# DeltaNet and a hard-swish MLP in one kernel: weight pieces loaded in one transfer or in several slabs

## The chip, the cores and the metric

The kernel runs on one core of a Trainium2 chip. A core has five engines, each with an instruction queue of its own: TensorE (PE, matrix products, with PEld for the loading of the stationary operand), VectorE (DVE), ScalarE (ACT), GpSimd (POOL) and SyncE (SP), which here does nothing but issue DMA transfers. The transfers run on 16 DMA engines. The time is that of the device in microseconds; the kernel before has a median of 661.7 us over three runs (661.16 to 663.97).

## The reference

Two parts in a row. The first is a delta-rule recurrence over 768 steps, for 4 batches of 8 heads of width 48; the second is an MLP over the 3072 tokens.

```python
for t in range(S):
    kt, vt, bt = (k_n[:, :, t], v[:, :, t], beta[:, :, t, None])
    y[:, :, t] = np.einsum('bhd,bhde->bhe', q[:, :, t], state)
    v_old = np.einsum('bhde,bhd->bhe', state, kt)
    state = state + bt[:, :, :, None] * np.einsum('bhd,bhe->bhde', kt, vt - v_old)
...
x = np.ascontiguousarray(attn_out.transpose(0, 2, 1, 3)).reshape(B * S, H * D)
h = x @ w_in                                   # (3072, 384) @ (384, 2048)
g = h * np.clip(h + 3.0, 0.0, 6.0) / 6.0
out = g @ w_out                                # (3072, 2048) @ (2048, 384)
```

`k_n` is k divided by its norm per token and head. q, k, v and beta are float32. The two weight matrices are float64 in memory, 8 bytes an element, and the kernel makes float32 of them itself.

## The kernel before

**The recurrence.** The 768 steps are cut into 24 chunks of 32 tokens. A tile has 128 rows: 32 tokens of each of the 4 batches. For each chunk k is normalised (`norms`: a square on ACT at L396, a sum on DVE at L402, and so on), k and q are transposed by PE (L513) and copied by ACT (L521, tile `KQ`), products of them become a triangular matrix (PE L536, DVE L547), which is inverted; for the first chunk `product` does that by matrix products (L585 and the lines around it), for groups of four chunks DVE does it column by column after a transposition (L458). Then the state is read, corrected and updated, and the output y of the chunk is turned into `xT`, the MLP's input.

**The MLP.** `up` multiplies two chunks (a block of 256 tokens) by w_in (L983), applies the activation, and `down` multiplies by w_out. Later blocks use variants with fewer products (L1055, L1215).

**The weights.** Both matrices are loaded in pieces, eight of w_in and eight of w_out, 768 KB of float64 each. Piece i of w_in is 256 columns of all 384 rows: 128 partitions, three row blocks (`s`), 256 columns. Piece i of w_out is two row blocks of 128 rows with all 384 columns. `load_w(i)` (L309) issues the transfer of piece i from SP at L320, into a home in `spare` or in a part of `w_out` that is not yet in use; pieces from 6 on reuse a home, and so wait until the piece that had it has been read. `scales` reads the raw halves of a piece on ACT in four operations (L345); `convert` reads them on DVE in three (L367, L372, L378) and writes float32. The first ACT operation and the first two DVE operations of a piece read the raw data; all of them take the whole piece at once. The MLP's first product (L983) needs the first pieces of w_in.

**The other loads.** For each chunk there are four transfers of 48 KB each for k (L168), q (L180) and v (L193), one for each batch, all issued from SP. The output is written from SP as well (L1140).

**What sets the order.** The first part of the program is emitted by the list `ORDER`, a hand-written sequence of words; each word takes one step of one generator: `w` issues the next weight piece, `k`, `q` and `v` one transfer of 48 KB, `a` one operation of `scales`, `c` one of `convert`, `n` of the norms, and so on. The order of the words is the order of each engine's queue. `W` is `w` with an added wait: `do` looks for the one instruction that the step emitted and has `behind_tensor` make it wait for the latest PE instruction before it. In the list, piece 12 alone is issued by `W`. After the list, a loop over the remaining chunks follows a plan of its own, with no weight loads in it.

The lines that the change touches are L320 to L322 in `load_w` and the few lines in `do` for the words K, Q, V and W.

Of the kernel before, what the change touches and what calls it, by code (L numbers as in the profile page):

```python
# [10 lines left out]
U32 = mybir.dt.uint32  # L11
# [33 lines left out]
def kernel(  # L45
# [21 lines left out]
    nc = tc.nc  # L67
# [27 lines left out]
    def rows(b):  # L95
        return slice(C * b, C * b + C)
# [4 lines left out]
    def group(t):  # L101
        return (0, t) if t < G0 else ((t - G0) // GS + 1, (t - G0) % GS)
# [34 lines left out]
    def needs(*what):  # L137
        assert past.issuperset(what), (what, set(what) - past)
# [70 lines left out]
    for j, value in enumerate((1.0, -1.0)):  # L209
        m = mask2[:, j, :]  # L210
        for b in range(B):
            nc.gpsimd.memset(mask2[rows(b), j, :], value)
            nc.gpsimd.affine_select(
                out=mask2[rows(b), j, :], in_=mask2[rows(b), j, :], pattern=[[1, C]],
# [88 lines left out]
    raws = []  # L303
    for i, n in enumerate((0, 1, 2, 3, 4, 5, 0, 1, 3, 4, 5, 0, 1, 5, 0, 1)):
        s, f = weights[i][0].shape[1:]
# [3 lines left out]
    def load_w(i):  # L309
        dst, src = weights[i]  # L310
        if src.dtype == FP32:
            if i >= NWI:
                needs(("w", NWI - 1))
            nc.sync.dma_start(out=dst, in_=src)
            past.add(("raw", i))
            return
        if i in frees:
            needs(("seen", frees[i], 0), ("seen", frees[i], 1))
        past.add(("raw", i))
        nc.sync.dma_start(  # L320
            out=raws[i].rearrange("p s f z -> p s (f z)"), in_=src.bitcast(U32)
        )  # L322

    es = [
        spare[:, 2, j : j + WP * NKT // 2].bitcast(U16).rearrange("p (s f) -> p s f", s=NKT)
# [1016 lines left out]
    def made(name, make, ok=True):  # L1342
        if name not in gens:
            gens[name] = make() if ok else iter(())
        return gens[name]

    def prep_of(t):
        return made(("p", t), lambda: prep(t), t < N)
# [7 lines left out]
    def inverse_of(g):  # L1356
        return made(
            ("i", g), lambda: halves_of(g) if g == 1 else inverse(g), g < NG
        )
# [6 lines left out]
    def pieces():  # L1366
        for i in range(NW):
            load_w(i)
            yield
# [37 lines left out]
    def behind_tensor(ins):  # L1407
        last = next(
            i for i in reversed(nc.cur_bb.bb.instructions) if i.engine == mybir.EngineType.PE
        )  # L1410
        tc.add_manual_dep(
            ins, last.name,
            mybir.DependencyInfo(mybir.DependencyClass.Sync, mybir.DependencyReason.DATA),
            reason="held back",
        )

    def do(word):
        if word in ("K", "Q", "V", "W"):
            n = len(nc.cur_bb.bb.instructions)
            next(gens[word.lower()])  # L1420
            (new,) = nc.cur_bb.bb.instructions[n:]
            behind_tensor(new)
        elif word in gens:
            next(gens[word])
        elif word[0] == "r":
            relus[word[1]].pop(0)()
        elif word[0] == "g":
            pending[word[1]].pop(0)()
        elif word == "e":
            evicts.pop(0)()  # L1430
        elif word[0] == "i":
            next(inverse_of(int(word[1:])), None)
        else:
            name, t = word[0], int(word[1:])
            if name == "p" and t >= LS + LE:
                next(prep_of(t), None)
            else:
                key = (name, t) if name in "hp" else ("early", name, t)
                next(made(key, lambda: makers[name](t)), None)

    with tc.manual_schedule():
        for word in ORDER.split():
            word, _, n = word.partition("*")
            for _ in range(int(n or 1)):
                do(word)
# [12 lines left out]
        for t in range(LS, N):  # L1458
            g, i = group(t)
# [94 lines left out]
```

## Time and profile before

| What | Value |
|---|---|
| median of three runs | 661.7 us (661.16, 661.7, 663.97) |
| the profiled execution | 662.71 us, of which its span 661.0 |
| PE busy | 632.6 us, 96% of the span |
| DVE, ACT, POOL busy | 499.5, 263.2, 226.6 us |
| transfers of weight pieces | 16 of 768 KB; median 4.9 to 7.0 us to landing, by group |
| transfers of k, q, v | 96 each, of 48 KB; median 3.0, 2.6, 2.5 us to landing |
| granted TensorE clock | mean 0.989; 0.50 in 32 to 40 us |

The span runs from the first to the last instruction. Times in the profile are in microseconds from its start. L12 is line 12 of the kernel. SPq is SP's queue, which is not counted as busy; for a transfer the profile gives the start and length of its issue, and for most the time from issue to landing. `spare<-in_moe_w_in_dram` is the transfer of a piece of w_in into the tile `spare`; the names kf, qb and vf are the tiles of k, q and v. In the slices, each digit is the busy share in tenths of one fortieth of the span.

### The profile page before, as it was taken

What the parts mean: (1) busy time and instruction counts of PE and PEld (TensorE: products, weight loads), DVE (VectorE), ACT (ScalarE), POOL (GpSimd) and SP (SyncE); (2) the same over time, 40 slices, a digit from 0 to 9 for tenths busy, and PEclk for the clock granted to TensorE, in tenths of its full rate; (3) what the DMA queues carried; (4) which work ended last, traced back from release to release, by engine and by line L of the source; (5) the groups of instructions that cost most, each with busy time, mean ns of one, the idle gap of its engine ahead of it and who ended that gap; (6) DMA issues with size and microseconds to landing.
All of it is one profiled execution on the core that took longest, in us unless ns stands there. A gap on an engine that the chain in (4) does not pass through costs nothing.

```text
span 661.0 us, 26631 instructions
## 1 busy us (share of the span) xinstructions
PE 632.6 (96%) x11640; PEld 568.8 (86%) x11640; DVE 499.5 (76%) x1164; ACT 263.2 (40%) x547; POOL 226.6 (34%) x352
## 2 busy tenths in 40 slices
PE   2768999999999999999999999999999999999997
PEld 2658987776689989999999999999999999999997
DVE  5899877798657988758988748979658998456354
ACT  4786578322232154154144244244244144153240
POOL 5531023003661354453254354164152241331330
PEclk9979999999999999999999999999999999999999
DMA  7888246212041030041030030030020020000101
GB/s 171 210 216 217 76 100 165 49 25 39 16 84 20 2 75 3 3 83 28 3 74 3 2 74 3 2 63 2 3 50 2 2 49 3 23 18 2 26 1 24
DMA packets 88692, 33.28 MB, mean 50 GB/s; under 512 B 80224, under 2 KB 83424, under 8 KB 88576
## 3 DMA queue, kind: packets, MB, share of 16 engines
q1 hardware_dynamic: 88224, 31.29, 21.5%
q8 instruction: 91, 1.49, 0.9%
q10 hardware_dynamic: 352, 0.30, 0.2%
q14 instruction: 25, 0.20, 0.1%
HBM read 26.84 MB, written 4.72 MB: 48 GB/s over the span
## 4 chain that ended last, share of the span: by engine, by line
PE 91%; DVE 3%; DMA 2%; ACT 2%; SPq 1%; issue 1%; ACTq 0%; DVEq 0%
PE po L1215 28%; PE ph L1055 27%; PE ph L983 9%; PE po L1151 6%; PE ks L795 4%; PE pz L816 3%; PE pt L513 3%; PE py L816 3%; PE su L927 3%; PE sc L536 3%; ACT spare L345 1%; PE yt L862 1%; DMA w_out<-in_moe_w_in_dram 1%; SPq L168 1%; PE pi L673 1%
## 5 line engine op out<-in xcount | busy, mean ns | idle before, releaser
L1055 PE MATMUL ph<-xT,w_in 128*128 128x128 f32 (+1 forms) x720 | 156.7, 321 | 0.2 <-issue 0.2
L1019 POOL TENSOR_TENSOR g<-g 128x256 f32<-128x256 f32 (+1 forms) x144 | 88.0, 612 | 105.5 <-ACT g L1069 99.9
L1055 PEld LDWEIGHTS ph<-xT,w_in 128*128 128x128 f32 x720 | 116.9, 191 | 6.7
L1215 PE MATMUL po<-w_out,g 128*128 128x192 f32 x640 | 110.6, 326 | 0.0
L1215 PEld LDWEIGHTS po<-w_out,g 128*128 128x128 f32 x640 | 104.6, 190 | 0.5
L1215 PE MATMUL po<-spare,g 128*128 128x192 f32 x480 | 86.7, 332 | 0.0
L1069 ACT ACTIVATE g<-ph 128x512 f32<-128x512 f32 x72 | 43.0, 597 | 107.5 <-PE ph L1055 107.5
L1215 PEld LDWEIGHTS po<-spare,g 128*128 128x128 f32 x480 | 77.2, 190 | 1.8
L983 PE MATMUL ph<-xT,w_in 128*128 128x128 f32 (+1 forms) x384 | 72.8, 339 | 1.5 <-ACT xT L866 0.6
L1225 POOL TENSOR_TENSOR o<-o,u 128x192 f32<-128x192 f32 x18 | 14.9, 828 | 163.5 <-ACT o L1222 76.1
L983 PEld LDWEIGHTS ph<-xT,w_in 128*128 128x128 f32 x384 | 60.2, 196 | 9.0 <-DVE g L993 0.9
L1082 DVE TENSOR_TENSOR g<-ph,g 128x256 f32<-128x256 f32 x72 | 30.2, 419 | 47.3 <-PE ph L1055 44.8
L748 DVE TENSOR_TENSOR pr<-A 128x30 f32<-128x30 f32 (+9 forms) x150 | 57.6, 384 | 3.3
L1201 DVE TENSOR_TENSOR g<-g 128x512 f32<-128x512 f32 x80 | 55.3, 712 | 3.6 <-PE po L1215 3.6
L1102 DVE SCALAR_TENSOR_TENSOR g<-o,g 128x512 f32<-128x512 f32 x72 | 52.5, 729 | 7.2 <-ACT o L1099 7.2
L753 DVE TENSOR_TENSOR A<-A,pr 128x30 f32<-128x30 f32 (+9 forms) x150 | 55.1, 367 | 3.3
L1055 PE MATMUL ph<-beta_tok,sums_in 128*128 128x128 f32 x288 | 55.9, 275 | 0.1
L1099 ACT ACTIVATE o<-g 128x512 f32<-128x512 f32 x72 | 45.4, 631 | 12.0 <-DVE g L1102 8.5
L345 ACT ACTIVATE spare<-spare 128x768 uint16<-128x768 uint16 (+1 forms) x56 | 47.3, 850 | 3.2 <-DMA kf<-in_k_dram 1.7
L499 POOL TENSOR_TENSOR kb<-kf,inv 128x384 f32<-128x384 f32 x24 | 21.7, 906 | 75.5 <-issue 42.6
L1222 ACT ACTIVATE o<-po 128x192 f32<-128x192 f32 x40 | 13.2, 330 | 83.2 <-PE po L1215 83.2
L1151 PE MATMUL po<-w_out,g 128*128 128x384 f32 x128 | 45.4, 490 | 0.0
(137 smaller groups left out, 1010.2 us busy)
## 6 DMA issues: line engine op xcount, KB each, us to landing
kf<-in_k_dram SPq DMA_DIRECT2D x96, 48.0 KB, 3.0
qb<-in_q_dram SPq DMA_DIRECT2D x96, 48.0 KB, 2.6
vf<-in_v_dram SPq DMA_DIRECT2D x96, 48.0 KB, 2.5
out_dram<-o SPq DMA_DIRECT2D x90, 48.0 KB, 1.6
spare<-in_moe_w_in_dram SPq DMA_DIRECT2D x4, 768.0 KB, 5.3
w_out<-in_moe_w_in_dram SPq DMA_DIRECT2D x4, 768.0 KB, 5.6
w_out<-in_moe_w_out_dram SPq DMA_DIRECT2D x4, 768.0 KB, 7.0
spare<-in_moe_w_out_dram SPq DMA_DIRECT2D x4, 768.0 KB, 4.9
```

The source lines that it names most:

```text
L345: nc.scalar.activation(out=z, in_=z if n else d.bitcast(I16)[:, :, :, 3], func=func, bias=value, scale=scale,)
L748: nc.vector.tensor_tensor(out=pv, in0=A[:, j + 1 :, j].unsqueeze(2).to_broadcast([n, w, j]), in1=A[:, j, 0:j].unsqueeze(1).to_broadcast([n ...
L753: nc.vector.tensor_tensor(out=A[:, j + 1 :, 0:j], in0=A[:, j + 1 :, 0:j], in1=pv, op=ALU.subtract)
L983: nc.tensor.matmul(ph[:, cols], lhsT=w_in[:, s, f * 128 : (f + 1) * 128], rhs=xT[:, s, cols], start=(s == 0), stop=(s == NKT - 1),)
L1019: nc.gpsimd.tensor_tensor(out=out, in0=a, in1=b, op=op)
L1055: nc.tensor.matmul(ph[:, n], lhsT=w, rhs=x, start=start, stop=stop, skip_group_check=True)
L1069: nc.scalar.activation(out=gt, in_=ph[:], func=ACTF.Copy)
L1099: nc.scalar.activation(out=r, in_=g, func=ACTF.Relu, bias=0.5, scale=1.0 / 6.0)
L1102: nc.vector.scalar_tensor_tensor(out=g, in0=r, scalar=1.0, in1=g, op0=ALU.min, op1=ALU.mult)
L1151: nc.tensor.matmul(pos[c][:], lhsT=gs[blk, f // 2][:, f % 2, c * P : (c + 1) * P], rhs=w_out[:, f, :], start=(f == 0), stop=(f == NFC - 1),)
L1201: nc.vector.tensor_tensor(out=A(f, *out, 4), in0=A(f, *a, 4), in1=A(f, *b, 4), op=op)
L1215: nc.tensor.matmul(ps[n][:], lhsT=A(f - f % 2, *a)[:, f % 2], rhs=b[:, f], start=(f == 0), stop=(f == HF - 1),)
```

## The change

`load_w` takes the views of destination and source that it had and issues one transfer for each index of their second dimension: three for a piece of w_in (one for each block of 128 rows, 256 KB each) and two for a piece of w_out (384 KB each). All go to SP's queue one after the other, within one step of the generator. `do` for the words with an added wait now gives that wait to each instruction that the step emitted. What is read afterwards, and the list `ORDER`, stay as they are.

```diff
         if i in frees:
             needs(("seen", frees[i], 0), ("seen", frees[i], 1))
         past.add(("raw", i))
-        nc.sync.dma_start(
-            out=raws[i].rearrange("p s f z -> p s (f z)"), in_=src.bitcast(U32)
-        )
+        dst, src = raws[i].rearrange("p s f z -> p s (f z)"), src.bitcast(U32)
+        for j in range(dst.shape[1]):
+            nc.sync.dma_start(out=dst[:, j], in_=src[:, j])
...
         if word in ("K", "Q", "V", "W"):
             n = len(nc.cur_bb.bb.instructions)
             next(gens[word.lower()])
-            (new,) = nc.cur_bb.bb.instructions[n:]
-            behind_tensor(new)
+            for new in list(nc.cur_bb.bb.instructions[n:]):
+                behind_tensor(new)
```

## The prediction

> **What bounds the kernel now.** I read the profile in this order: the slices of the page, the chain of waits, the timeline of SP's queue, the landings of single transfers, and the timelines of DVE and ACT where a weight piece is first read. The slices come first, because they say where time can be lost at all.
>
> ```profile
> PE   2768999999999999999999999999999999999997
> DVE  5899877798657988758988748979658998456354
> ACT  4786578322232154154144244244244144153240
> DMA  7888246212041030041030030030020020000101
> ```
>
> A slice is 16.5 us. From the fifth slice on PE is 9 throughout, so nothing that the loads do there matters unless a load is very late. In the first four slices (66 us) PE is at 2, 7, 6 and 8, while the DMA engines are at 7 to 8 and DVE at 5 to 9: this is the only stretch in which the change can act. All sixteen pieces are issued by 103 us, the eight of the first matrix by 44.2 us. The chain of waits says what sets the pace there.
>
> ```profile
> 7.49 5.07 DMA spare<-in_moe_w_in_dram
> 12.58 0.31 SPq L180
> ...
> 15.42 6.95 DMA w_out<-in_moe_w_in_dram
> 22.46 0.93 ACT spare L345
> ...
> 40.96 0.84 ACT spare L345
> 41.80 1.47 ACT KQ L521 x3
> ...
> 46.75 1.88 DVE A L458
> ```
>
> Columns are start, length and what it was. Pieces 0 and 2 are on the chain themselves; then ACT's scaling of the pieces (L345), then DVE, then PE to the end. Piece 0 is issued at 7.49 and lands 5.07 later, at 12.56, and in the same instant SP's queue goes on (12.58). SP's own timeline shows why:
>
> ```profile
> 7.49 0.45 SPq L320 DMA_DIRECT2D spare<-in_moe_w_in_dram  x1
> 7.99 2.95 SPq L168 DMA_DIRECT2D kf<-in_k_dram  x6
> 10.98 0.45 SPq L320 DMA_DIRECT2D spare<-in_moe_w_in_dram  x1
> 12.58 0.31 SPq L180 DMA_DIRECT2D qb<-in_q_dram  x1
> ...
> 32.44 3.87 SPq L180 DMA_DIRECT2D qb<-in_q_dram  x5
> 36.35 0.45 SPq L168 DMA_DIRECT2D kf<-in_k_dram  x1
> 36.91 1.28 SPq L320 DMA_DIRECT2D spare<-in_moe_w_in_dram  x1
> ```
>
> The transfer at 12.58 is the eighth after piece 0, and it starts when piece 0 has landed; the same holds at 22.39, 26.52, 31.57 and 43.79. So at most eight transfers of this queue are under way, and a ninth waits for the landing of the one eight places earlier. An issue costs 0.45 us, and the next starts 0.49 after it. Last, the piece that is read the moment it lands:
>
> ```profile
> 42.85 0.96 DVE L378 SCALAR_TENSOR_TENSOR w_in<-spare 128x768 f32<-128x768 f32 x1
> 43.87 0.56 DVE L367 TENSOR_SCALAR spare<-spare 128x768 uint32<-128x768 uint32 x1
> ...
> 43.86 3.56 ACT L345 ACTIVATE spare<-spare 128x768 uint16<-128x768 int16 x4
> ```
>
> Piece 6 is issued at 36.91 and takes 6.87 (the landing of that one transfer, 6.9 in the view of line 320), so it is there at 43.78. DVE ends the work before at 43.81 and reads it at 43.87; ACT ends at 43.75 and reads it at 43.86. It has no slack, and behind it on DVE stand the four products of L547 and the transposition at 46.75, which is on the chain.
>
> **The change, part by part.** *Removed:* sixteen issues of 768 KB. *Added:* eight times three and eight times two, 40 in all, so 24 more issues; the bytes stay. A weight piece's rows are 2 KB (first matrix) or 3 KB (second) in memory and go as such already: the page counts 5,152 packets between 2 and 8 KB, and 8 x 384 + 8 x 256 is 5,120 of them. So packets stay too, and only their grouping and order change.
>
> *SP's time up to piece 6.* From 7.49 to 36.91 SP issues 45 transfers: 45 x 0.49 = 22.0, so 7.4 of the 29.4 us are stalls. Five are waits for a landing (1.15 before 12.58, 0.47 before 16.34, 1.69 before 22.39, 0.85 before 26.52, 1.11 before 31.57: 5.3), and long issues make 2.4 (1.90 for two at 16.34, 3.87 for five at 32.44, where 0.49 each would do). Six pieces of three parts put 12 issues more in front of piece 6: 57 x 0.49 = 27.9. With every stall kept, its first part starts 5.9 later (42.8); if the stalls take up all of it, nothing. I walk the first stall to choose. The third part of piece 0 is issued at 8.47 and its data cannot be there before 12.5 (a piece takes 4.5 at the least, and it is the same data). Eight places behind it now stands the second part of piece 1: that goes at 12.58, the third at 13.07, the q transfer at 13.56, which is 0.98 later than before, of 1.96 added. One stall takes one piece's worth. Later ones take less: they end with landings that are now late themselves, and an issue that runs long does so at its own times, wherever the queue then stands, so that those that fell into a wait before now hit an issue. Going on in this way through the queue I keep 5.8 of the 7.4 us of stalls, and the first part of piece 6 is issued at 7.49 + 27.9 + 5.8 = 41.2, the last at 42.2.
>
> *Its landing.* The rows give 4.5, 5.3 and 6.9 us (least, median, most) from issue to landing of such a piece in the home that piece 6 uses. Parts issued 0.49 apart are quicker issued than moved, so I count the piece from its first part: 45.7, 46.5 or 48.1. I take the median, since the 6.9 of before holds a long issue of its own (1.28 for 0.45): 46.5, which is 2.7 later than 43.78.
>
> *Its readers.* ACT's L345 and DVE's L367 wait for three landings instead of one. An added wait is one instruction of 0.02 us on the sequencer (L367's five are 21 ns each), fourteen for seven pieces on two engines, and some 0.01 to 0.03 for the hand-over: 0.2 at most is on the path, taken whole. Behind L345 stand the copies KQ (L521), for which PE waits; behind L367 the products L547.
>
> *Pieces before it.* Piece 0 lands when it did (above). Piece 2, read at 22.46 after 0.42 of waiting, is issued about 3 later, but its data has to queue behind piece 1 anyway; I give it 0.3, inside the 2.7 and not on top, since delays of one in-order chain are not added but the greatest counts. Piece 3 has 0.9 of slack to ACT (26.51 against 27.39), piece 5 about 1; both shift less than piece 6's readers.
>
> *Pieces after it.* Piece 7 lands near 49.3 and is first read at 52.12; its readers shift by the same amount. The second matrix adds eight issues, 3.9 us of SP; they are covered by SP's idle time (7.9 us held behind a matmul at 65.4, 3.4 before 77.18, 4.2 before 92.86) and by the pieces' slack (piece 8 lands at 53.1 and is read by ACT at 56.69). Without that cover they cost up to 3.9. Piece 12 alone is held behind a product of PE: both its parts get that wait, the second finds it met; the v transfer behind it goes 0.49 later and has waits of its own. I cost this group at nothing.
>
> *Sum.* 2.7 + 0.2 = 2.9 us, all at DVE before 47 us; from there the chain runs through DVE and PE, which is idle for 0.9 us in all from 64 to 120 us, to the end, so it arrives there. On the profiled execution (span 661.0, 662.71 in all) that is 665.6; that execution stands 1.0 over the median of 661.7, so the forecast is 664.6.
>
> **A rule against it.** The row: one piece of 768 KB alone lands in 4.5 us, a 48 KB load in 1.9, and 48 KB loads under way together land 0.27 apart (13.40 and 13.95 for two). The Trainium skill (DMA: Bandwidth & Descriptors, Bandwidth) says that transfers should be 1 MiB or more and that small ones pay mostly overhead. By its fit of 2.0 us plus bytes at 436 GB/s a piece is 3.8 and three parts one after another 7.8, an estimate from that page; the parts overlap here, by the 0.27, so the sum does not take it.
>
> **The rivals.** *Each part also costs the DMA engines a start.* Priced by the nearest row, the 0.27 that a small load under way takes, 12 added parts hold up piece 6 by 3.2 more: 2.9 + 3.2 = 6.1, 667.8. For it: DMA share is 1.01 in both stretches from 8 to 24 us, so anything added there is late. Against: the 0.27 is mostly that load's own data, which parts do not add. *Hidden.* The stalls take up all the added issues, pieces land as before, and 0.2 remains: 661.9. For it: 7.4 us of stalls against 5.9 of issues, and the split leaves packets as they are. Against: the DMA share falls to 0.71 from 32 to 40 us, so there the queue and not the data sets the landing. *Faster.* A piece holds one of eight places for 5 to 7 us; a part gives its place back earlier, and the first slab can be moved while the next is issued. If this makes pieces land sooner than the added issues make them later, DVE and ACT wait less. It decides at piece 0, landing before 12.56. The price is bounded by DVE's idle time between 12 and 44 us: 1.4, 0.8, 0.5, 0.3 and 0.2, together 3.3, so 658.4 at the best and 659.6 for two thirds. Against: piece 0's 24 packets on each engine must come anyway, and the queue has more to issue. *Clock.* PE is busy 0.14 of the 2 us from 46, and the granted clock is 0.50 from 50 to 52; a longer gap could lengthen that half-speed stretch by as much again, 3.4 us, and cost up to 1.7 where PE is on the path. This is an add-on to the forecast (its top), not a case.
>
> **How the numbers follow.** Forecast 0.50, at 664.6, with its own range from 663.0 (landing in 4.5 and half a microsecond more taken up) to 666.7 (landing in 6.9, or the clock). Start per part 0.22, hidden 0.18, faster 0.10. The range from 660.8 to 668.6 has at its top what is found if no stall takes anything up (5.9 and the 0.98 of piece 6's own parts, 661.7 + 6.9), and leaves out most of the faster case. About 0.5% (3.3 us) is what a measurement of this kernel can tell from no change: slower means over 665.0. That is the start per part and somewhat under half of the forecast (0.22): 0.44. Faster means under 658.4, half of that case: 0.05. Within it is 0.51.
>
> **What would show it.** In the changed profile: 40 issues on the weights' line with 0.45 each; piece 6's first part near 41 and DVE's L367 on it near 46.7 instead of 43.87, with a wait for a DMA before it; PE's first up-projection (48.99 before) some 3 later; from 66 us on the same PE time. A piece 6 that is read before 45 makes the hidden case true; a first piece that lands after 13 the start per part; one that lands before 12.4 the faster one. Wrong altogether would be a loss that arises after 66 us.

## The result, and the profile after

| | before | after |
|---|---|---|
| median of 6 runs each, taken together | 662.13 us (661.16 to 664.11) | 666.92 us (665.95 to 667.75) |
| the profiled execution's span | 661.0 us | 665.6 us |
| PE busy | 632.6 us | 636.5 us |
| mean granted clock | 0.989 | 0.979 |

The ratio is 1.0053, that is 3.5 us, with a 95% interval of 1.0034 to 1.0072, or 2.3 to 4.8 us. The plain medians differ by 4.8 us, which is the upper end of that interval, and the spans of the two profiled executions by 4.6. The forecast was 2.9 more than before, inside the interval. The changed kernel is slower, by about the 0.5% that can be told from no change.

The slices of the page after the change (PE, DVE, PE's clock, DMA; a slice is 16.6 us):

```profile
PE   2768999999999999999999999999999999999997
DVE  4879887799648988858988858988758998456354
...
PEclk9957999999999999999999999999999999999999
DMA  6769237402042030032030030030020020010101
```

From the fifth slice on nothing has changed for PE. In the first four the DMA digits are 6, 7, 6, 9 where they were 7, 8, 8, 8: the same bytes (31.29 MB on that queue in both) move later. The table of stretches of the changed kernel (stretch; sum; PE, PEld, DVE, ACT and POOL busy us with instruction counts; granted clock, DMA share, GB/s) narrows it down:

```profile
32.00:40.00 8.00, 6.33 (x200) 5.27 (x196) 7.07 (x23) 4.50 (x7) 3.36 (x5) 0.50 0.79 190
40.00:48.00 8.00, 4.66 (x101) 3.65 (x92) 5.27 (x8) 5.64 (x9) 1.12 (x1) 0.50 0.69 168
48.00:56.00 8.00, 6.60 (x176) 5.84 (x164) 7.21 (x20) 4.24 (x7) 2.26 (x5) 0.50 0.91 254
```

In 40 to 48 us DVE has 8 instructions and is busy for 5.27 us (13 and 7.77 before), ACT 9 and 5.64 us (12 and 7.53 before), PE 101 (205 before). That is where the time goes. SP's queue shows what it was doing there (columns: start, length of the issues, line, tiles, number):

```profile
33.46 1.32 SPq L180 DMA_DIRECT2D qb<-in_q_dram  x1
35.23 0.31 SPq L168 DMA_DIRECT2D kf<-in_k_dram  x1
35.58 1.45 SPq L322 DMA_DIRECT2D w_out<-in_moe_w_in_dram  x3
37.07 3.23 SPq L180 DMA_DIRECT2D qb<-in_q_dram  x5
40.34 0.45 SPq L168 DMA_DIRECT2D kf<-in_k_dram  x1
41.25 1.75 SPq L322 DMA_DIRECT2D spare<-in_moe_w_in_dram  x3
```

The line of weights is now L322. Piece 5 has its three parts at 35.58, 36.08 and 36.55 (one issue at 31.93 before), piece 6 at 41.25, 42.18 and 42.57 (36.91 before). And the readers, ACT first (in brackets the idle time before it and what ended it):

```profile
42.27 0.91 ACT L345 ACTIVATE spare<-w_out 128x768 uint16<-128x768 int16 x1 [3.05 <-DMA kf<-in_k_dram]
43.21 2.59 ACT L345 ACTIVATE spare<-spare 128x768 uint16<-128x768 uint16 x3
45.71 2.04 ACT L521 ACTIVATE KQ<-pt 128x512 f32<-128x512 f32 x4
47.62 3.57 ACT L345 ACTIVATE spare<-spare 128x768 uint16<-128x768 int16 x4
51.09 0.47 ACT L850 ACTIVATE y<-py 128x384 f32<-128x384 f32 x1
52.56 0.49 ACT L866 ACTIVATE xT<-yt 128x384 f32<-128x384 f32 x1 [0.99 <-PE yt L862]
```

The first of these is ACT's read of piece 5. L345 reads nothing of k; the bracket names the k load that was issued at 40.34, eight places behind the first part of piece 5, and so a transfer of the same place in SP's round of eight. Piece 5's own third part landed at about 42.18: SP is ready for piece 6's second part at 41.64 and issues it at 42.18, and the transfer eight places ahead of it is that third part. ACT stood idle for 3.05 us for it; before, it read piece 5 at 38.27, directly behind its work. Of these 4.0 us, 3.65 are the later first issue (35.58 for 31.93). Everything behind it on ACT moves by about as much: the copies KQ from 41.71 to 45.71, y (L850) from 47.33 to 51.09, and with xT PE's first up-projection, from 48.99 to 53.10. DVE:

```profile
42.29 0.56 DVE L367 TENSOR_SCALAR spare<-w_out 128x768 uint32<-128x768 uint32 x1 [0.28 <-DMA kf<-in_k_dram]
42.88 0.96 DVE L372 SCALAR_TENSOR_TENSOR spare<-w_out,spare 128x768 f32<-128x768 uint32 x1
45.83 0.96 DVE L378 SCALAR_TENSOR_TENSOR w_in<-spare 128x768 f32<-128x768 f32 x1 [1.99 <-ACT spare L345]
46.86 0.56 DVE L367 TENSOR_SCALAR spare<-spare 128x768 uint32<-128x768 uint32 x1
...
48.60 0.42 DVE L547 TENSOR_TENSOR L<-sc,mb 128x256 f32<-128x256 f32 x1 [0.19 <-PE sc L536]
```

DVE waits 1.99 us in the middle of piece 5, for ACT's half of it. It reads piece 6 at 46.86 (43.87 before), directly behind its own work, and then waits 0.19 for PE, which has waited 2.58 for ACT's copies. ACT too comes to piece 6 straight from KQ, so that neither reader waits for piece 6. In the chain of waits the stretch from 42 to 59 us now runs over ACT and then PE, where before it went over to DVE at 45.34:

```profile
40.34 1.94 DMA kf<-in_k_dram
42.28 0.91 ACT spare L345
...
45.71 1.08 ACT KQ L521 x3
...
47.75 0.83 ACT spare L345
...
51.19 0.39 ACT y L850
...
53.10 4.21 PE ph L983 x18
```

### The profile page after: what moved, and what is told of

It reads as the page before. It is cut to its first block, busy times and chain, and to the rows that moved or that the text cites. A ratio compares the mean times of both kernels' runs of the same rounds, so it can differ in the third digit from the quotient of the medians.

```text
span 665.6 us, 26673 instructions
## 1 busy us (share of the span) xinstructions
PE 636.5 (96%) x11640; PEld 571.6 (86%) x11640; DVE 500.5 (75%) x1164; ACT 263.1 (40%) x547; POOL 226.8 (34%) x352
## 3 DMA queue, kind: packets, MB, share of 16 engines
q1 hardware_dynamic: 88608, 31.29, 21.4%
q8 instruction: 91, 1.49, 1.0%
## 4 chain that ended last, share of the span: by engine, by line
PE 92%; DMA 2%; SPq 2%; ACT 1%; DVE 1%; issue 1%; ACTq 0%
PE po L1215 28%; PE ph L1055 27%; PE ph L983 10%; PE po L1151 6%; PE ks L795 4%; PE pz L816 3%; PE pt L513 3%; PE py L816 3%; PE su L927 3%; PE sc L536 2%; PE yt L862 1%; ACT spare L345 1%; PE pi L673 1%; DMA spare<-in_moe_w_in_dram 1%; SPq L168 1%
## 5 line engine op out<-in xcount | busy, mean ns | idle before, releaser
L345 ACT ACTIVATE spare<-spare 128x768 uint16<-128x768 uint16 (+1 forms) x56 | 47.5, 852 | 3.8 <-DMA kf<-in_k_dram 2.7
L499 POOL TENSOR_TENSOR kb<-kf,inv 128x384 f32<-128x384 f32 x24 | 21.7, 907 | 76.0 <-issue 42.6
```

What stands on the lines that cost most here:

```text
L345: nc.scalar.activation(out=z, in_=z if n else d.bitcast(I16)[:, :, :, 3], func=func, bias=value, scale=scale,)
```

## The experiments

Three explanations were open. *Queue*: the added issues, each with a place among SP's eight, make pieces 5 and 6 start late. *Start per part*: each part costs the DMA engines something of its own. *Clock*: PE at half speed (31.57 to 58.88 us in one stretch after the change; 31.96 to 42.2 and 49.03 to 52.44 before) is a cause and not a consequence. Times of runs are medians of 5 to 12 executions, against 17 to 29 of the kernel before in the same comparison; the ratio is to these, and need not be exactly that of the two medians. The columns from the profile are of one execution each. "Ahead" counts the issues that SP has more than before in front of piece 6; the two next columns are ACT's first read of piece 5 and PE's first up-projection in the profiled execution.

| run | ahead | ACT reads 5 | first up | span | ratio (95%) |
|---|---|---|---|---|---|
| before | 0 | 38.27 | 48.99 | 661.0 | |
| second matrix alone | 0 | 37.80 | 48.49 | 659.2 | 1.0014 (0.9999 to 1.0030) |
| pieces 4 to 7 | 4 | 38.73 | 49.62 | 662.5 | 1.0018 (1.0001 to 1.0035) |
| two parts | 6 | 38.57 | 50.42 | 662.1 | 1.0003 (0.9989 to 1.0016) |
| pieces 0 to 3 | 8 | 39.66 | 51.21 | 662.9 | 1.0024 (1.0012 to 1.0037) |
| first matrix alone | 12 | 41.06 | 51.55 | 664.8 | 1.0052 (1.0033 to 1.0071) |
| the change | 12 | 42.27 | 53.10 | 665.6 | 1.0053 (1.0034 to 1.0072) |
| whole pieces, unread loads | 12 | 43.24 | 54.51 | 666.7 | 1.0087 (1.0070 to 1.0104) |
| the change, 8 q loads on GpSimd | 4 | 37.01 | 47.87 | 661.8 | 1.0023 (1.0007 to 1.0039) |
| before, 8 q loads on GpSimd | -8 | 40.26 | 54.71 | 665.3 | 1.0059 (1.0036 to 1.0082) |
| parts on GpSimd | 0 | 41.55 | 57.05 | 669.5 | 1.0108 (1.0092 to 1.0124) |
| split pieces earlier | moved | 41.72 | 52.21 | 664.8 | 1.0034 (1.0018 to 1.0051) |
| whole pieces earlier | moved | 39.33 | 51.22 | 663.3 | 1.0010 (0.9996 to 1.0024) |
| split pieces earlier, behind v | moved | 39.00 | 52.84 | 664.1 | 1.0050 (1.0032 to 1.0069) |

**One matrix at a time.** The loop over the parts is kept for the pieces of one matrix only, the first (below), or the second (with `i >= NWI`):

```diff
-        for j in range(dst.shape[1]):
-            nc.sync.dma_start(out=dst[:, j], in_=src[:, j])
+        if i < NWI:
+            for j in range(dst.shape[1]):
+                nc.sync.dma_start(out=dst[:, j], in_=src[:, j])
+        else:
+            nc.sync.dma_start(out=dst, in_=src)
```

> Only the eight pieces of the first matrix are split in three; the second matrix is loaded as before. Theory 1 (SP's 16 added issues before 50 us make pieces 5 and 6 land late, and ACT and DVE wait for them): the whole loss is here, 3.5 to 5 us over the kernel before, DVE's first read of piece 6 at 46 to 47.5 us. Theory 2 (the parts cost the DMA engines starts of their own, for every piece of either matrix): some two thirds of the loss, 2.5 to 3.5 us. Theory 3 (the second matrix's added issues hold up later k, q and v loads): under 1.5 us.

> Only the eight pieces of the second matrix are split in two. Theory 1: within 0.7 us of the kernel before, since SP is idle between these loads and their readers come late. Theory 2: 1 to 2 us slower. Theory 3: 3 us slower or more.

The first matrix alone: 665.75 us against 662.44, by the ratio the whole loss. ACT's read of piece 5 says why:

```profile
41.06 0.91 ACT L348 ACTIVATE spare<-w_out 128x768 uint16<-128x768 int16 x1 [2.94 <-DMA w_out<-in_moe_w_in_dram]
```

(The scaling is L348 in this kernel.) Here the bracket names the piece itself. Piece 6 is read by DVE at 45.69, again directly behind its work. The second matrix alone: 663.3, 0.9 above, with an interval that just touches no change, and a span 1.8 below that of the profiled execution before. Its pieces cost little or nothing.

**The issues without the parts.** Whole pieces as before; behind each piece of the first matrix SP issues two transfers of 256 bytes into a tile that nothing reads. This kernel loads 4 KB more than it needs.

```diff
         nc.sync.dma_start(
             out=raws[i].rearrange("p s f z -> p s (f z)"), in_=src.bitcast(U32)
         )
+        if i < NWI:
+            for j in range(2):
+                c = slice(8 * i + 4 * j, 8 * i + 4 * j + 4)
+                nc.sync.dma_start(out=unread[0:16, c], in_=src.bitcast(U32)[0:16, 0, 0:4])
+
+    unread = const.tile([128, 8 * NWI], U32, name="unread")
```

> Every piece is loaded in one transfer, as before; behind each of the eight pieces of the first matrix stand two added transfers of 256 bytes each into a tile that nothing reads. They take SP's issue time and two of the eight places, and hardly any data time. Theory 1: most of the loss of the split, 2.5 to 5 us, with piece 6 first read by DVE after 45.5 us. Theory 2: under 1 us. Theory 3: under 0.7 us.

667.95 against 662.44: 5.5 us, more than the change, and its profiled execution has the clock at 1.000 throughout. So neither parts of weight pieces nor half speed are needed for the loss: small transfers on the same queue are enough. SP's queue of this kernel shows what they take, issues and places:

```profile
36.71 0.45 SPq L320 DMA_DIRECT2D w_out<-in_moe_w_in_dram  x1
37.20 0.94 SPq L326 DMA_DIRECT2D unread<-in_moe_w_in_dram  x2
38.19 3.06 SPq L180 DMA_DIRECT2D qb<-in_q_dram  x5
43.18 0.31 SPq L168 DMA_DIRECT2D kf<-in_k_dram  x1
43.62 0.39 SPq L320 DMA_DIRECT2D spare<-in_moe_w_in_dram  x1
```

The k load is the eighth transfer behind piece 5 (two unread, five q, itself), and it stands from 41.25 to 43.18. In the chain of waits of this kernel piece 5 lands in that instant:

```profile
36.71 6.46 DMA w_out<-in_moe_w_in_dram
43.16 0.02 issue
43.18 0.02 ACTq L351
...
43.24 0.93 ACT spare L351
```

Piece 6 is issued only at 43.62, and ACT and DVE read it near 49.03 (43.86 before). Before the eighth transfer behind each of pieces 0 to 5 SP stood for 1.1 to 1.9 us, 8.6 in all. That it is worse than the change, with the same number of issues, fits the places: here the whole piece holds its place until all of it has landed, and the split gives two of three back sooner (the first part of piece 5 landed 3.94 us after its issue, piece 5 here took 6.45). That point was not tried by itself.

The unread loads are transfers too, so by themselves they don't rule out that each added transfer costs the DMA engines a start. The pages' lines on the loads' queue bear on that (packets, MB, share of the 16 engines' span; the kernel before, then the changed one):

```profile
q1 hardware_dynamic: 88224, 31.29, 21.5%
q1 hardware_dynamic: 88608, 31.29, 21.4%
```

The split adds 384 packets, 16 for each of the 24 added transfers, where the prediction had none. They are of 4 bytes, and in the trace such a packet takes 9 ns: 384 of them over 16 engines are 0.2 us in the whole kernel. The time of all packets stays as it was: 21.5% of 661.0 us is 142.1, and 21.4% of 665.6 is 142.4 (between executions the share goes from 20.6 to 21.7% here, in no order of the transfers added). So the added transfers hardly give the engines more to do. A delay in which the engines move nothing would not show in these numbers.

**How many issues.** As in the diff for one matrix, with `if i < 4` (pieces 0 to 3) or `if 4 <= i < NWI` (pieces 4 to 7) in place of `if i < NWI`; and with all of the first matrix in two parts, two row blocks and then one, the second matrix whole (the condition `if i < NWI` stays, and only its loop differs):

```diff
-            for j in range(dst.shape[1]):
-                nc.sync.dma_start(out=dst[:, j], in_=src[:, j])
+            for r in (slice(0, 2), slice(2, 3)):
+                nc.sync.dma_start(out=dst[:, r], in_=src[:, r])
```

> Only pieces 0 to 3 are split in three; the others are loaded whole. Theory 1: eight of the twelve issues ahead of piece 6 stay, so piece 6 lands 1 to 2.5 us later than before and the loss is 1 to 2.5 us. Theory 2: piece 5 and 6 are whole and land as before but for what piece 3 leaves over; under 1 us.

> Only pieces 4 to 7 are split in three; 0 to 3 and the second matrix are whole. Ahead of piece 6 this adds 4 issues (1.96 us without stalls), half of what splitting pieces 0 to 3 adds. Queue theory: piece 6's first part 1 to 2 us later than 36.91, DVE's first read of it 0.5 to 2 us later than 43.87, time 0.5 to 2 us over the kernel before. Start-per-part theory: the four pieces around the read have all their parts, so it costs as much as splitting all eight (3 to 4 us).

> Pieces of the first matrix go in two parts (two row blocks and one), those of the second whole: eight added issues before 50 us instead of sixteen, six instead of twelve ahead of piece 6. Theory 1 (added issues of SP's queue): about half of what the split in three loses (3.3 us in the run with the first matrix alone), 1 to 2.5 us. Theory 2 (each part costs the DMA engines a start): half of it too, so this run measures a size and does not part the two.

663.71 against 662.44, 664.27 against 663.51, and 663.76 against 663.54. By the ratios four issues ahead cost 0.18% (0.01 to 0.35), six nothing that can be told, eight 0.24%, twelve 0.5%. That fits stalls that take up the first of them, as the prediction had it for piece 1. Pieces 4 to 7 split have all the parts that are on the way when pieces 5 and 6 are read, and cost 1.2 us by the ratio, 2.3 at most, where the start per part was to cost 3 to 4: against it. The run with pieces 0 to 3 also shows a limit of a single profile: PE's state update (L930) waits 2.29 us before 41.88 for nothing that the profile shows, and DVE's piece 5 stands behind it, so not all of its 1.96 us at DVE is the queue's.

**Issues taken off SP, parts kept.** Two of the q chunks, eight transfers that stand ahead of piece 6, are issued from GpSimd; first in the changed kernel, then in the kernel before.

```diff
-            for _ in load_q(t):
+            for _ in load_q(t, nc.gpsimd if t in (2, 3) else nc.sync):
```

> The changed kernel, but the eight transfers of q for chunks 2 and 3 are issued by GpSimd instead of SP: eight of the twelve issues that the split puts ahead of piece 6 are taken away from SP again. Theory 1: 1.5 to 3 us faster than the changed kernel, so 1 to 3 us over the kernel before. Theory 2: as slow as the changed kernel, 4 to 5 us over.

> The kernel before with the same eight q transfers on GpSimd's queue. Theory 1: pieces 4 to 6 land earlier, and the kernel is 0.5 to 2 us faster than before (DVE waits 3.3 us in all between 12 and 44 us). Theory 2: no change.

With the split, 664.68 against 663.54: by medians 1.1 us over the kernel before, where the change is 4.8 over it; by ratios 1.5 and 3.5 (the two intervals, 0.07 to 0.39% and 0.34 to 0.72%, just overlap). In the timelines of SP and DVE of that kernel:

```profile
30.96 2.20 SPq L322 DMA_DIRECT2D w_out<-in_moe_w_in_dram  x3
...
36.22 2.15 SPq L322 DMA_DIRECT2D spare<-in_moe_w_in_dram  x3
```

```profile
42.17 0.96 DVE L378 SCALAR_TENSOR_TENSOR w_in<-spare 128x768 f32<-128x768 f32 x1
43.17 0.56 DVE L367 TENSOR_SCALAR spare<-spare 128x768 uint32<-128x768 uint32 x1
```

Pieces 5 and 6 are issued 4.6 and 5.0 us earlier than after the change, and DVE reads piece 6 at 43.17, 0.7 before the kernel before, with all 24 added transfers still there. This is the reverse test: the parts stay, eight of the issues leave SP, and the lateness at piece 6 goes with them. In this profile, 0.8 us longer than that before, what remains arises later: DVE is still 0.70 ahead at 60 us and 0.04 at 83.

In the kernel before the same move was to gain and lost 3.8 us (667.36 against 663.54): a miss. Its pieces are issued early (piece 6 at 34.23), but PE waits longer, by its list of waits (us in total, times, longest):

```profile
PE pt L513 <- POOL kb L499: 7.9, 1, 7.9
PE sc L536 <- issue: 5.4, 3, 2.1
...
PE su L927 <- issue: 1.2, 1, 1.2
```

The first line is 8.3 before. The others are new: "issue" is time in which PE waited for nothing that the profile shows, and before it was 0.3 for each of two groups from 40 to 85 us. DVE stands 2.52 us for PE's sc at 51.30. The DMA share in 24 to 40 us is 1.11 and 1.09 (0.87 and 0.71 before), and the page lists a queue of instructions (91 packets) on the same DMA engines; that the full engines starve PE of instructions is a guess that no run tests. So the move has a cost of its own, and how much of it is in the split kernel's 1.1 us stays open.

**Parts on another queue.** The second and third part of each piece of the first matrix go out from GpSimd:

```diff
         for j in range(dst.shape[1]):
-            nc.sync.dma_start(out=dst[:, j], in_=src[:, j])
+            eng = nc.gpsimd if j and i < NWI else nc.sync
+            eng.dma_start(out=dst[:, j], in_=src[:, j])
```

> The changed kernel, but the second and third part of each piece of the first matrix are issued by GpSimd's queue instead of SP's. The parts are the same, SP has 16 issues fewer before 50 us. Theory 1: the loss goes, to within 1 us of the kernel before, unless GpSimd's own work ahead of the pieces' readers holds the parts up. Theory 2: the loss stays, 3 us or more, with weight data as slow as in the changed kernel.

670.81 against 663.54, the slowest of all. It doesn't tell the theories apart, since the parts only changed queues: GpSimd issues piece 6's at 43.85, behind products of its own, one of which waits 3.42 us for PE, and DVE then reads the piece at 51.64.

**The order of the queue.** If the queue sets the time, moving pieces 5 and 6 up in the list should win it back. Piece 5's step goes ahead of a v, a q and a k load, piece 6's ahead of five q and a k load (of each line of the list only the part that changes is shown):

```diff
-m3 v c p2 n4*2 q p2 k c b2 h0 c h0 w a*2 h0
-p4*2 a*2 m4 p3 q*4 h0 q k w p4*2
+m3 w v c p2 n4*2 q p2 k c b2 h0 c h0 a*2 h0
+p4*2 a*2 m4 p3 w q*4 h0 q k p4*2
```

> All pieces stay split as in the change (40 weight issues on SP's queue); in the order list piece 5's step is put ahead of the three loads (v, q, k) that it followed, and piece 6's ahead of the six (five q, one k). Queue theory (the change loses time because the added issues make pieces 5 and 6 start late): piece 5's first part near 33 us instead of 35.58, piece 6's near 37.4 instead of 41.25, DVE's first read of piece 6 at 43 to 44.5 instead of 46.86, and the time comes back to between 0 and 2 us over the kernel before, unless the delayed q loads (3 us later) become the next wait, which would show as a wait of PE or ACT on q. Start-per-part theory (each part costs the DMA engines a start wherever it stands): the number of parts is the same, so the time stays 4 to 5 us over the kernel before.

> The kernel before (whole pieces) with the same two steps moved up. Queue theory: ACT's wait of 1.7 us for piece 5 before 38.27 shrinks, DVE's first read of piece 6 comes at 43 to 43.8 (43.87 before), and the time is between 1 us below and 1 us above the kernel before, since DVE was not waiting there. If the moved q loads are the next wait, it is 1 to 3 us slower.

Split: 665.65 against 663.51. By the ratio that is 2.3 us over the kernel before, where the change is 3.5 over it and 0 to 2 were expected; the two intervals overlap, so that a part is won back is not clear of noise. PE's timeline shows what stands in the way:

```profile
39.81 1.49 PE L816 MATMUL pz<-vf,X 32*32 32x48 f32 x58 [3.15 <-DMA vf<-in_v_dram]
```

The v load that now stands behind piece 5 (35.00) is the next wait. With whole pieces, 664.23 against 663.51, no difference that can be told: PE waits 1.4 us for the same v load. The wait of 1.7 us for piece 5 that the expectation names is not in the kernel before, where ACT reads piece 5 directly behind its work. So the last run puts that load ahead of piece 5 again (shown against the run before, again in part):

```diff
-m3 w v c p2 n4*2 q p2 k c b2 h0 c h0 a*2 h0
+m3 v w c p2 n4*2 q p2 k c b2 h0 c h0 a*2 h0
```

> As the run with the split pieces moved up, but the one v load that had come to stand behind piece 5 is put ahead of it again; piece 5 still goes ahead of one q and one k load, piece 6 ahead of five q and one k. Queue theory: with the 3.2 us wait of PE for that v load gone (39.81 in that run), DVE ends its state update before 42 us, DVE's first read of piece 6 is at 43.2 to 44.5 and the time is 0 to 2 us over the kernel before (the change itself: 4 to 5 over it). If the order of the loads isn't what sets the time and the split itself costs it wherever the loads stand, it stays 3 us or more over the kernel before.

666.1 against 663.55: a miss in the number. The wait for v is gone, and another has taken its place:

```profile
41.53 0.45 PE L927 MATMUL su<-R,sums_in 32*64 32x48 f32 x3 [1.44 <-issue]
41.91 1.12 PE L513 MATMUL pt<-ident,kb 128*128 128x128 f32 x4
44.80 1.94 PE L513 MATMUL pt<-ident,qb 128*128 128x128 f32 x8 [1.77 <-DMA qb<-in_q_dram]
```

Now it is q, whose five loads are issued from 38.30 to 42.22 behind piece 6 (37.07 to 40.30 after the change, with a wait of 0.32). DVE reads piece 6 at 45.13, but its product L547 comes at 48.72, 2.03 late for PE. By the number alone this run would also fit a cost that stays wherever the loads stand; the bracket on q, the eight q loads taken off the queue above, and the packets' time that the split leaves as it was, speak for the queue. No run here is faster than the kernel before.

## Why the prediction was right, and which piece it had wrong

*SP's queue.* Forecast: first part of piece 6 at 41.2, last at 42.2. It was 41.25 and 42.57. Two of the terms were off and cancelled, which is luck: the queue started piece 0 at 6.65 and not at 7.49 (two issues of 0.83 us in the profiled execution before were shorter here), and the stalls kept were 6.7, not 5.8.

*Landing of piece 6.* Forecast 46.5; its last part landed at 46.73. Forecast for DVE's read 46.7; it was 46.86. The agreement of the read is in part luck as well. The sign was a wait for a DMA before it, and there is none: DVE comes from its product for piece 5, which ends at 46.79 because it stood 1.99 us for ACT's half of that piece. With piece 6 there at 44 it would have been read at 46.86 all the same.

*The rest of the way.* Here the mechanism is the right one and the piece the wrong one. The sum has 2.9 "all at DVE before 47 us; from there the chain runs through DVE and PE" to the end, and says of piece 5 that it has "about 1" of slack and shifts less than piece 6's readers. Piece 5 was the worse of the two: ACT's first read of it shifts by 4.0 (38.27 to 42.27), DVE's of piece 6 by 2.99. The term that was mis-sized is piece 5's. The prediction's own chain of waits has it: L345 at 40.96, ahead of KQ, is ACT's last operation on piece 5. The piece takes ten of the twelve issues that piece 6 gets in front of it, its last part included twelve, and its last part landed some 5.6 us after its issue. ACT, in order, then carries those 4 us through KQ, piece 6 and y to the first up-projection (+4.11), past DVE, whose transposition is 3.48 late. So the sum was to be made for both engines, and its greatest term was 4.1 in this execution and not 2.9.

How much that is varies from one execution to the next. In the profile of the first matrix alone, with the same twelve issues ahead, ACT's read of piece 5 is 2.79 late, DVE's of piece 6 is 1.82 late and the first up-projection 2.56. So piece 5 leads in both, and no reader waits for piece 6 in either; but that the forecast was too small as a number rests on one execution and on medians at the end of their interval. The rest, to 4.6, comes between 60 and 83 us, where DVE's delay grows from 4.05 to 4.70. The runs don't settle it: in the same stretch it changes by -1.0 (second matrix alone), 0.0 (earlier, behind v), +0.6 (unread loads) and +1.1 (first matrix alone).

*Cover of the later pieces.* Costed at nothing; the second matrix alone measured 0.9 (0.0 to 0.3%), and in its one profile DVE was 0.75 early at 60 us. Right within what can be told.

*The rivals.* Start per part: its 667.8 is nearer to the median of 666.92 than the forecast. Its sign, a first piece that lands after 13, did not come: SP goes on behind piece 0's third part at 12.81. That alone decides little, since the piece was issued 0.84 earlier and took 6.2 us from its first issue, against 5.07 before. But in the five other runs whose SP issues piece 0 in three parts it took 5.1 to 5.7 until SP went on, as the whole piece did in six. With that, the packets' time, the four split pieces around the read and the q loads taken off the queue decide against it as the cause. The rule on large transfers that the prediction weighed (the Trainium skill, DMA: Bandwidth & Descriptors, Bandwidth) agrees in direction only. The price by the page's fit, 3.8 against 7.8 us for a piece, isn't what was paid. (The page gives that fit, under Anatomy of one DMA, as measured for transfers issued from GpSimd; these go out from SP.) The parts of pieces 5 and 6 whose landing is recorded took 3.9 and 4.2 us from their issue, and all of piece 5 was there 6.6 us after its first issue, where the whole piece took at most 6.3 before. What was paid is SP's time. Hidden: six issues ahead can't be told from none, twelve can. Faster: no split beat whole pieces. Clock: the half-speed stretch did grow, to 27.3 us, but the unread loads lose more at full clock, so it isn't needed. Nor does the clock move the time of the kernel before: of its 95 executions in these comparisons, the 30 with a mean clock below 0.985 have a median of 662.8 us, the 33 at 0.99 or more 663.5.

## What to carry to other kernels

Where one queue issues every load, count what a split adds in issues and in places under way, and walk it to each late reader, not only to the one with no slack: the piece ahead of it, on the other engine that reads it, can set the end. The chain of waits before the change names that piece, if each of its rows is put down to the piece that it works on. Here six issues ahead, which SP's stalls could take up, could not be told from none, and twelve cost about 3.5 us. When such a queue is full, a reordered load only hands the wait on, here from a weight piece to v and then to q.

## What the hardware showed that was not expected

Issues on SP that run long (up to 1.78 us for 0.45) made up 4.4 of the 6.7 us of stalls after the change, against 2.4 before. Those of over 1 us end about 0.4 us after the end of a 16 KB packet of the instruction queue (91 packets and 1.49 MB in either profile). That is a coincidence in time that no run varied.

An issue from GpSimd takes 0.55 to 0.75 us there, and eight of them off SP's queue recovered about 3.7 of 4.8 us by medians, 2.0 of 3.5 by ratios. The Trainium skill (DMA: Bandwidth & Descriptors, Issuing engines are not separate DMA queues) says that a second issuing engine saves only the time of initiating, usually small relative to the transfer. The mechanism agrees; the size doesn't here, since up to 43 us the issues of SP's queue set when pieces 5 and 6 start.
